# Gate weights of the first mixture: three tiles looked up first, all of them two tiles later

## The chip, the cores and the metric

The kernel runs on one core of a Trainium2 chip. The metric is the device time of one execution in microseconds; before the change it is 932.36 us, the median of 3 runs (931.68 to 932.57). TensorE (PE) multiplies matrices, VectorE (DVE), ScalarE (ACT) and GpSimd (POOL) work element by element, and SyncE (SP) issues most transfers. Each engine has a queue of its own and executes it in the order in which it is written; engines wait for each other by semaphores.

## The reference

Three layers follow each other over 2304 tokens of 512 numbers: an attention in which each row keeps only scores within tau of its maximum, and two mixtures of eight experts. Only the first mixture matters here:

```python
logits = x @ w_gate
e_idx = np.argmax(logits, axis=1)
probs = softmax(logits)                       # over the 8 experts
gate_w = probs[np.arange(N), e_idx]
eom = 1.0 / (1.0 + np.exp(-(x @ w_output_gate)))
for e in range(E):
    mask = e_idx == e
    h = np.maximum(x[mask] @ w1[e], 0.0)
    out[mask] = gate_w[mask, None] * eom[mask, e, None] * (h @ w2[e])
```

So each token goes to one expert, and its result is scaled by one number, the product of two gates.

## The kernel before

Attention fills the first third of the program. Near its end the routing of the first mixture is computed: for each token its expert and its rank among that expert's tokens, and from these its place in a list that is sorted by expert and cut into tiles of 128 places (`NT1=25` tiles at most, each of one expert). The tokens stand in 21 columns of 128 (`NC`; column 15 is empty).

Places are looked up with one-hot matrices on TensorE. For a column of tokens, `OB` says which of the 128 rows of a tile a token goes to, and `OA` which of the 25 tiles; twenty matmuls, one for each filled column, add up in PSUM to a value for every place (`onehots`, line 169). `OA` has three parts beside each other, so that three values are looked up at once (75 columns): at first the two halves of the token number and a one. So that the gathers can start early, the first three tiles are looked up from a small one-hot tile, `O3` (9 columns), before the big one (lines 151 to 154).

The first mixture (`moe1`, line 560) works tile by tile. For tile t the rows of x are gathered and transposed (`xT`), multiplied with the first weights (`mm1`, into H), passed through relu, transposed again (`hT`), multiplied with the second weights (`mm2`, into Y), scaled by the gates (`ey`, line 665, which also stores them), and transposed for the logits of the second mixture (`yT`, `logits`). Precision is kept by splitting each number into a rounded part and a rest (`xh` and `xl`, `wh` and `wl`); ScalarE rounds, VectorE (now and then POOL) subtracts, and three matmuls replace one. The tiles are interleaved: in the pass for tile t stand half of `mm1(t+1)`, `ey(t-1)`, `hT(t)`, the other half of `mm1(t+1)`, `yT(t-1)`, `xT(t+2)` and then `mm2(t)`, with the weight splits between them (lines 730 to 762). The kernel is scheduled by hand: the order in which the code runs is the order of every queue. There is one PSUM buffer for Y, so `mm2(t)` can't start until `ey(t-1)` has read it, and three for all transposes and lookups (`psT`).

The gates are computed while the first tiles run. `gates` (line 209) is a generator in three parts: exponentials and sums, right after the first tile's `mm1`; the quotient `gr`, and its split into three bf16 numbers `gb`, in the pass for tile 0; and in the pass for tile 1, ahead of `hT(1)`, the conversion of `gb` into PSUM and the three products that put the gate values into `OA` (lines 227 and 228). Later in the same pass, `gather_gates` does twenty lookups of 75 columns and adds the three parts (line 234). Then `rts.close()` gives back the routing's memory, the buffers for y are opened, and `ey(0)` scales tile 0.

Of the kernel before, what the change touches and what calls it, by code (L numbers as in the profile page):

```python
# [9 lines left out]
F32 = mybir.dt.float32  # L10
F32R = mybir.dt.float32r
BF16 = mybir.dt.bfloat16
I32 = mybir.dt.int32
AF = mybir.ActivationFunctionType
ALU = mybir.AluOpType
AX = mybir.AxisListType
ET = mybir.EngineType
P = 128
NT1 = 25
GL = 2  # L20
NC = 21
# [21 lines left out]
class Route:  # L43
# [8 lines left out]
    def T(self, nm, sh, dt=F32):  # L52
        return self.p.tile([P]+sh,dt,name=nm)
# [35 lines left out]

    def part(self, c0, c1, H=None):  # L90

# [7 lines left out]
        wt=self.wt8; vt=self.vtok[:,c]  # L99
        if H is not None:  # L100
            wt=H[:,0:8]; vt=H[:,8:8+n]; mx=H[:,32:32+n]; m2=H[:,64:64+n]
            V.tensor_copy(wt,self.wt8); V.tensor_copy(vt,self.vtok[:,c])
        def choose():
# [5 lines left out]
            V.tensor_mul(oh,t0,B8(vt))  # L109
            if H is not None: V.tensor_copy(self.mx[:,c],mx)  # L110
        def ahead(rtile):
            R[0]=rtile()[:,:8*n+8].rearrange("p (c e) -> p c e",e=8)
            for a in range(c0): nc.tensor.matmul(R[0],K['onesb'],self.oh[:,a:a+1].to_broadcast([P,n+1,8]),start=a==0,stop=False,skip_group_check=True)
# [21 lines left out]
    def tiles(self, rtile, p, mid):  # L135

        nc=self.nc; V=nc.vector; K=self.K; cst=self.cst; T=lambda nm,sh,dt=F32: p.tile([P]+sh,dt,name=nm)
        t1=T("ft1",[NC,8]); V.tensor_mul(t1,self.oh[:,:NC],self.bs.unsqueeze(1).to_broadcast([P,NC,8]))
        a=self.m2; V.tensor_reduce(a,t1,axis=AX.X,op=ALU.add)
        V.tensor_add(a,a,self.q)  # L140
        self.ix=cst.tile([P,NT1],I32,name="ix1"); self.vs=cst.tile([P,NT1],F32,name="vs1"); self.ix0=self.ri[:,:3]
        def hot(OA,n):
            B=lambda x: x.unsqueeze(2).to_broadcast([P,NC,n])
            V.tensor_tensor(OA[:,:,2],K['iota'][:,:n].unsqueeze(1).to_broadcast([P,NC,n]),B(a),op=ALU.is_equal)
            yield
            for i in range(2): V.tensor_mul(OA[:,:,i],OA[:,:,2],B(self.tok[:,i]))
            yield
        def token(ix,IX,n):
            fx=T(f"fx{n}",[n]); V.tensor_copy(fx,IX[:,1])
            V.scalar_tensor_tensor(ix,IX[:,0],16.0,fx,op0=ALU.mult,op1=ALU.add)  # L150
        O3=T("O3",[NC,3,3],BF16); h3=hot(O3,3); next(h3); next(h3)
        I3=self.onehots(rtile,O3,3)
        h=hot(self.OA,NT1); next(h)
        token(self.ix0,I3,3)

        f8=T("f8",[8]); f1=T("f1",[1]); ce=self.ce; self.tab0=self.ab[:,0,:2]
        V.tensor_scalar(f8,ce,ce[:,0:1],None,op0=ALU.is_le)
        V.tensor_scalar(self.tab0[:,1:2],ce[:,0:1],ce[:,7:8],None,op0=ALU.is_lt)
        V.tensor_reduce(f1,f8,axis=AX.X,op=ALU.add)
        V.tensor_scalar_min(self.tab0[:,0:1],f1,7.0)  # L160
        mid()
        next(h)
        IX=self.onehots(rtile,self.OA,NT1)
        tb=self.table(T); next(tb)
        token(self.ix,IX,NT1)
        V.tensor_copy(self.vs,IX[:,2])
        next(tb)
# [41 lines left out]
    def gates(self, rtile):  # L209

        nc=self.nc; V=nc.vector; T=self.T; n=NC; OA=self.OA
        dd=T("dd",[n,8]); V.tensor_sub(dd,self.LG[:,:,0:8],self.mx.unsqueeze(2).to_broadcast([P,n,8]))
        og=T("og",[n,8]); V.tensor_mul(og,self.oh[:,:n],self.LG[:,:,8:16])
        nc.scalar.activation(dd,dd,AF.Exp)
        ogs=T("ogs",[n]); V.tensor_reduce(ogs,og,axis=AX.X,op=ALU.add)
        sg=T("sg",[n]); nc.scalar.activation(sg,ogs,AF.Exp,scale=-1.0)
        yield
        se=T("se",[n]); V.tensor_reduce(se,dd,axis=AX.X,op=ALU.add)
        V.tensor_scalar_add(sg,sg,1.0)
        V.scalar_tensor_tensor(se,se,1e-9,sg,op0=ALU.add,op1=ALU.mult)  # L220
        gr=T("gr",[n]); V.reciprocal(gr,se)
        gb=T("gb",[3,n],BF16)
        for i in range(3):
            V.tensor_copy(gb[:,i],gr)
            if i<2: V.tensor_sub(gr,gr,gb[:,i])
        yield
        H=rtile()[:,:3*n].rearrange("p (i t) -> p i t",i=3); V.tensor_copy(H,gb)
        for i in range(3): V.tensor_mul(OA[:,:,i],OA[:,:,2],H[:,i].unsqueeze(2).to_broadcast([P,n,NT1]))
        yield

    def gather_gates(self, rtile):

        GX=self.onehots(rtile,self.OA,NT1); self.gs=self.cst.tile([P,NT1],F32,name="gs")
        self.nc.vector.tensor_reduce(self.gs,GX.rearrange("p i t -> p t i"),axis=AX.X,op=ALU.add)


def attention(tc, K, route, q, k, v, tau, wg, wo, xd, yz, preload):
    nc=tc.nc
    ident=K['ident']; NB=4; DIRECT=4; LG=route.LG
    with ExitStack() as ctx, ExitStack() as early:  # L240
# [293 lines left out]
        rank(); hot()  # L534
        choose,ahead,count,rank,hot=route.part(16,NC,psS.tile([P,2,512],F32,tag="S",name="H")[:,0])
        early.close()
# [23 lines left out]
def moe1(tc, K, r, rts, xd, w1, w2, wg2, ys, LG2, reach_, ahead):  # L560
# [4 lines left out]
    with ExitStack() as ctx:  # L565
# [30 lines left out]
        rtile=lambda: psT.tile([P,512],F32,tag="T",name="Tr")  # L596
# [16 lines left out]
        def gather(t):  # L613
            x=xp.tile([P,512],F32R,tag="x",name="x"); X[t]=x
            nc.gpsimd.indirect_dma_start(out=x.bitcast(F32),out_offset=None,in_=xd,in_offset=bass.IndirectOffsetOnAxis(ap=(r.ix0 if t<3 else ix)[:,t:t+1],axis=0))
# [21 lines left out]
        def relu(t):  # L637
            H=Hs.pop(t)
            h=hp.tile([P,8,P],F32,tag="h",bufs=1,name="h")
            for i in range(2): nc.scalar.activation(h[:,4*i:4*i+4],H[:,i],AF.Relu)  # L640
            Hs[t]=h
# [28 lines left out]
        def yT(t,b,i):  # L670
            y=X.pop(t)
            p=psT.tile([P,4,P],F32,tag="T",name="Ty")
            for c in range(4): nc.tensor.transpose(p[:,c],y[:,c*P:(c+1)*P],ident)
            if i==0: YT[b]=yp.tile([P,4,GL,P],F32,tag="yT",bufs=2,name="yT")
            nc.scalar.copy(YT[b][:,:,i],p)
# [35 lines left out]
        def splits(ahead):  # L711

            nonlocal pos
            while pos<min(used+ahead,ends[cur[0]]):
                t,c=order[pos]; pos+=1
                if c==0: regload(t)
                if t==0 and c<6: prefetch(t,c)
                else: split(t,c)
# [4 lines left out]
        gates=r.gates(rtile); pre=None  # L723
        splits(5); relu(0)
        next(gates)
        cnt=yp=WG=gs=None
        def run(j):
            nonlocal cnt,yp,WG,gs,pre
            t0,t1=runs[j]; lb=None; cur[0]=j; top=[]
            for t in range(t0,t1):  # L730
                i=(t-t0)%GL; b=t-i; nx=t+1<t1
                if t==t0 and j>0: splits(7); mm1(t,0,4); relu(t)
                early=t==1
                splits(5 if early else 7)
                if nx: mm1(t+1,0,2)
                if early: next(gates)
                elif t>t0: ey(t-1)
                if len(top) in (1,3): top.pop(0)()
                late=hT(t,early)
                splits(4 if early else 7)  # L740
                if t==0: next(gates)
                if nx: mm1(t+1,2,4); relu(t+1)
                if early:
                    r.gather_gates(rtile); gs=r.gs
                    rts.close()
                    yp=pool("yp",3); WG=yp.tile([P,4,32],F32,name="WG",bufs=1)
                    nc.gpsimd.memset(WG,0.0); nc.sync.dma_start(WG[:,:,:8],wg2.rearrange("(c p) e -> p c e",p=P))
                    ey(0); late(); splits(4)
                elif t>t0: yT(t-1,b if i else b-GL,(i-1)%GL)
                if t+3<N: gather(t+3)  # L750
                if t+2<N: xT(t+2)
                if lb is not None: logits2(lb,GL); lb=None
                splits(8 if nx else 7)
                end=j==0 and t==t1-1
                if end: lb=b-GL; logits(lb,GL)
                mm2(t)
                if early: yT(0,0,0)
                if t>t0 and i==0 and not end: lb=b-GL; logits(lb,GL)
                if end: pre=ahead(r.ix,r.vs,rtile)
                if j==0 and t==t1-4: top=list(reach(b-GL))  # L760
                if len(top) in (2,4,5): top.pop(0)()
                if j==0 and t==15: cnt=nc.values_load(tab[0:1,5,0:1],min_val=1,max_val=N)
            ey(t)
            if j+1<len(runs):
                with tc.If(cnt>t1,preferred_fallthrough_block=False): run(j+1)
            yT(t,b,i)
            if lb is not None: logits2(lb,GL)
            if j==0: logits1(t); next(pre)
            else: logits(b,i+1); logits2(b,i+1)
# [361 lines left out]
```

## Time and profile before

| | |
|---|---|
| median of 3 runs | 932.36 us (931.68 to 932.57) |
| profiled execution | 930.74 us, span of its instructions 928.6 us |
| mean granted TensorE clock | 0.982 of full speed |
| PE busy | 879.3 us, 95% of the span |
| DVE / ACT / POOL busy | 698.1 / 632.6 / 272.8 us |
| first mixture, from the first `mm1` | 336.1 us into the span |
| second mixture's first matmul | 692.2 us |

The profile is of one execution. Times in the rows are microseconds from the start of the span. A timeline row has start, duration, engine, line, operation, output<-inputs and the number of instructions merged into it; in square brackets how long the engine stood idle before it and what ended that. PE rows are matmuls, whose ends are modelled, so successive starts say more than durations; PEld rows are the loads of their weights.

### The profile page before, as it was taken

What the parts mean: (1) busy time and instruction counts of PE and PEld (TensorE: products, weight loads), DVE (VectorE), ACT (ScalarE), POOL (GpSimd) and SP (SyncE); (2) the same over time, 40 slices, a digit from 0 to 9 for tenths busy, and PEclk for the clock granted to TensorE, in tenths of its full rate; (3) what the DMA queues carried; (4) which work ended last, traced back from release to release, by engine and by line L of the source; (5) the groups of instructions that cost most, each with busy time, mean ns of one, the idle gap of its engine ahead of it and who ended that gap; (6) DMA issues with size and microseconds to landing.
All of it is one profiled execution on the core that took longest, in us unless ns stands there. A gap on an engine that the chain in (4) does not pass through costs nothing. (4 is left out here: it accounts for less than half of the span.)

```text
span 928.6 us, 18051 instructions
## 1 busy us (share of the span) xinstructions
PE 879.3 (95%) x5939; PEld 732.7 (79%) x5939; DVE 698.1 (75%) x1232; ACT 632.6 (68%) x1070; POOL 272.8 (29%) x350
## 2 busy tenths in 40 slices
PE   7899999999999999999999999997879999999995
PEld 6677777777777667888888888885449999999994
DVE  5998888889888789888888888887855555555540
ACT  5787878987877677888888888882324555455541
POOL 4234424432341421332233332331040222122211
PEclk9999999999999999999999999998779999999998
DMA  7534544444432572145543654112445665666400
GB/s 194 151 90 115 126 118 118 129 113 113 116 85 64 189 265 70 58 161 194 193 145 137 218 191 159 47 35 62 157 143 179 197 204 171 194 192 195 158 27 25
DMA packets 69346, 127.64 MB, mean 137 GB/s; under 512 B 14912, under 2 KB 27200, under 8 KB 69248
## 3 DMA queue, kind: packets, MB, share of 16 engines
q1 hardware_dynamic: 64016, 109.91, 38.7%
q0 software_dynamic: 5232, 16.52, 5.7%
q8 instruction: 49, 0.80, 0.4%
q14 instruction: 49, 0.40, 0.1%
HBM read 159.70 MB, written 15.99 MB: 189 GB/s over the span
## 5 line engine op out<-in xcount | busy, mean ns | idle before, releaser
L611 DVE TENSOR_TENSOR wl<-raw,wh 128x1024 fp32r<-128x1024 f32 x156 | 187.9, 1256 | 23.7 <-ACT wh L609 21.2
L609 ACT CAST wh<-raw 128x1024 fp32r x178 | 175.8, 1068 | 0.6 <-DMA raw<-in_moe_w_dram 0.4
L469 ACT ACTIVATE e<-S,nm 128x576 f32<-128x576 f32 x144 | 107.6, 748 | 55.1 <-DVE nm L464 54.7
L464 DVE TENSOR_REDUCE nm<-S 128x1 f32<-128x576 f32 x144 | 108.4, 757 | 21.9 <-PE S L388 11.2
L499 DVE SCALAR_TENSOR_TENSOR a<-S,th,e 128x576 f32<-128x576 f32 x144 | 114.4, 814 | 11.0 <-ACT e L469 4.7
L610 POOL TENSOR_TENSOR wl<-raw,wh 128x1024 fp32r<-128x1024 f32 x22 | 63.4, 2882 | 197.4 <-ACT wh L609 91.1
L966 DVE TENSOR_TENSOR wl<-raw,wh 128x1024 fp32r<-128x1024 f32 x60 | 73.4, 1225 | 36.8 <-ACT wh L966 36.8
L397 PE MATMUL T<-ident,a 128*128 128x128 f32 x576 | 86.6, 273 | 0.0
L1008 PE MATMUL H<-xh,wh 128*128 128x288 f32 x256 | 77.8, 304 | 0.1
L1020 PE MATMUL Y<-hh,wh 128*128 128x288 f32 x256 | 77.6, 303 | 0.0
L419 PE MATMUL O<-aT,v 128*64 128x288 f32 x512 | 75.8, 419 | 0.5 <-ACT xt L424 0.5
L633 PE MATMUL H<-wh,xh 128*128 128x512 f32 x184 | 75.1, 408 | 0.9 <-ACT xh L621 0.9
L1009 PE MATMUL H<-xl,wh 128*128 128x288 f32 x256 | 75.7, 296 | 0.2 <-DVE xl L1002 0.2
L1021 PE MATMUL Y<-hl,wh 128*128 128x288 f32 x256 | 75.6, 295 | 0.0
L1022 PE MATMUL Y<-hh,wl 128*128 128x288 f32 x256 | 75.5, 295 | 0.0
L1010 PE MATMUL H<-xh,wl 128*128 128x288 f32 x256 | 75.4, 294 | 0.0
L402 ACT COPY aT<-T 128x512 f32<-128x512 f32 x128 | 75.1, 587 | 0.2 <-PE T L397 0.2
L660 PE MATMUL Y<-wh,hh 128*128 128x512 f32 x184 | 73.9, 401 | 0.9 <-DVE y L667 0.9
L1037 POOL DMA_INDIRECT out_dram<-o,it x24 | 22.4, 932 | 173.1 <-ACT o L1031 154.2
L635 PE MATMUL H<-wh,xl 128*128 128x512 f32 x184 | 72.2, 392 | 0.0
L662 PE MATMUL Y<-wh,hl 128*128 128x512 f32 x184 | 71.9, 391 | 0.0
L634 PE MATMUL H<-wl,xh 128*128 128x512 f32 x184 | 71.7, 390 | 0.0
(344 smaller groups left out, 2089.4 us busy)
## 6 DMA issues: line engine op xcount, KB each, us to landing
raw<-in_moe_w_dram SPq DMA_DIRECT2D x256, 512.0 KB
ys<-y SPq DMA_DIRECT2D x23, 256.0 KB
q<-in_q_dram SPq DMA_DIRECT2D x16, 256.0 KB
k<-in_k_dram SPq DMA_DIRECT2D x16, 256.0 KB
v<-in_v_dram SPq DMA_DIRECT2D x16, 256.0 KB
QA<-QH SPq DMA_DIRECT2D x32, 128.0 KB
QB<-QH SPq DMA_DIRECT2D x32, 128.0 KB
xd<-xr SPq DMA_DIRECT2D x16, 256.0 KB
```

The costliest lines, as they stand in the source:

```text
L397: for kb in (2*part,2*part+1): nc.tensor.transpose(TT[n][:,kb,:],a[:,o+kb*P:o+(kb+1)*P],ident)
L419: nc.tensor.matmul(O[hd*64:hd*64+64,:288],L['v'][:,hd,kb,:],aT[hd][:,kb,cs],start=kb==0,stop=False,skip_group_check=True)
L464: nc.vector.tensor_reduce(nm[:,i:i+1],S[i][:,:,:288],axis=AX.XY,op=ALU.max,negate=True)
L469: nc.scalar.activation(e[i],S[i][:,:,:288],AF.Exp,bias=nm[:,i:i+1])
L499: nc.vector.scalar_tensor_tensor(a[:,hd*576:hd*576+576].rearrange("p (a b) -> p a b",a=2),S[i][:,:,:288],th[:,i:i+1],e[i],op0=ALU.is_ge,op ...
L609: nc.scalar.copy(h,rv(c,q['a']))
L611: else: nc.vector.tensor_sub(l,rv(c,q['v']),h.bitcast(F32))
L1008: nc.tensor.matmul(H[:,:288],wh[:,fs],xh[:,kc],start=kc==0,stop=False)
L1009: nc.tensor.matmul(H[:,:288],wh[:,fs],xl[:,kc],start=False,stop=False)
L1020: nc.tensor.matmul(Y[:,:288],wh[:,ds_],h,start=f==0,stop=False)
L1021: nc.tensor.matmul(Y[:,:288],wh[:,ds_],l,start=False,stop=False)
L1022: nc.tensor.matmul(Y[:,:288],wl[:,ds_],h,start=False,stop=f==7)
```

## The change

`O3` is no longer a tile of its own in memory that ends with attention, but a view of `t0`, a scratch tile of the routing that lives until `rts.close()`. The third part of `gates` becomes two: first the conversion and the three products on `O3` (3 tiles, 63 elements a row), and, when asked again, the conversion and the three products on `OA` (25 tiles, 525 elements). `gather_gates` takes the one-hot tile and its number of tiles and returns the scales. In the pass for tile 1 only those of tiles 0 to 2 are looked up (9 columns a matmul); in the pass for tile 3, behind `yT(2)`, both steps for all tiles follow each other directly, and the routing's memory is given back there.

```diff
-        O3=T("O3",[NC,3,3],BF16); h3=hot(O3,3); next(h3); next(h3)
+        O3=self.O3=self.t0.rearrange("p a b -> p (a b)").bitcast(BF16)[:,:9*NC].rearrange("p (c i t) -> p c i t",c=NC,i=3); h3=hot(O3,3); next(h3); next(h3)
...
-        H=rtile()[:,:3*n].rearrange("p (i t) -> p i t",i=3); V.tensor_copy(H,gb)
-        for i in range(3): V.tensor_mul(OA[:,:,i],OA[:,:,2],H[:,i].unsqueeze(2).to_broadcast([P,n,NT1]))
-        yield
-
-    def gather_gates(self, rtile):
-
-        GX=self.onehots(rtile,self.OA,NT1); self.gs=self.cst.tile([P,NT1],F32,name="gs")
-        self.nc.vector.tensor_reduce(self.gs,GX.rearrange("p i t -> p t i"),axis=AX.X,op=ALU.add)
+        for O,m in ((self.O3,3),(OA,NT1)):
+            H=rtile()[:,:3*n].rearrange("p (i t) -> p i t",i=3); V.tensor_copy(H,gb)
+            for i in range(3): V.tensor_mul(O[:,:,i],O[:,:,2],H[:,i].unsqueeze(2).to_broadcast([P,n,m]))
+            yield
+
+    def gather_gates(self, rtile, O, n):
+
+        GX=self.onehots(rtile,O,n); gs=(self.p if n<NT1 else self.cst).tile([P,n],F32,name=f"gs{n}")
+        self.nc.vector.tensor_reduce(gs,GX.rearrange("p i t -> p t i"),axis=AX.X,op=ALU.add)
+        return gs
...
                 if early:
-                    r.gather_gates(rtile); gs=r.gs
-                    rts.close()
+                    gs=r.gather_gates(rtile,r.O3,3)
...
                 elif t>t0: yT(t-1,b if i else b-GL,(i-1)%GL)
+                if t==3: next(gates); gs=r.gather_gates(rtile,r.OA,NT1); rts.close()
```

On VectorE in the pass for tile 1, before: the last weight subtraction, the conversion, three products on `OA`, the subtraction for the first half of h, the reduction `gs`, and the scaling of Y.

```order
L611 TENSOR_TENSOR wl<-raw_4552,wh 128x1024 [waits DMAHW5_49,Activation_49]
L227 CAST Tr<-gb 128x63 [waits DVE_49]
L228 TENSOR_TENSOR OA<-OA,Tr 128x21x25 [waits DVE_49]
L228 TENSOR_TENSOR OA<-OA,Tr 128x21x25
L228 TENSOR_TENSOR OA<-OA,Tr 128x21x25 [waits DVE_49]
L650 TENSOR_TENSOR hl<-Th,hh 128x512 [waits Activation_49]
L234 TENSOR_REDUCE gs<-Tr 128x25 [waits PE_49]
L667 TENSOR_SCALAR y<-Y,gs 128x512 [waits DVE_49]
```

The same place now; `t_930` is `t0` as the small one-hot tile.

```order
L613 TENSOR_TENSOR wl<-raw_4552,wh 128x1024 [waits DMAHW5_49,Activation_49]
L228 CAST Tr<-gb 128x63 [waits DVE_49]
L229 TENSOR_TENSOR t_930<-t_930,Tr 128x21x3 [waits DVE_49]
L229 TENSOR_TENSOR t_930<-t_930,Tr 128x21x3
L229 TENSOR_TENSOR t_930<-t_930,Tr 128x21x3 [waits DVE_49]
L652 TENSOR_TENSOR hl<-Th,hh 128x512 [waits Activation_49]
L235 TENSOR_REDUCE gs_5282<-Tr 128x3 [waits PE_49]
L669 TENSOR_SCALAR y<-Y,gs_5282 128x512 [waits DVE_49]
```

The instructions are as many and in the same order; only their shapes are smaller. In the pass for tile 3, VectorE's queue has these rows now: two weight subtractions, the conversion, the products on `OA`, the reduction, and the subtraction for x of tile 5. Before, the last of them came straight behind the second subtraction.

```order
L613 TENSOR_TENSOR wl<-raw_4555,wh 128x1024 [waits DMAHW7_49,Activation_49]
L607 TENSOR_LOAD tab
L613 TENSOR_TENSOR wl<-raw_4548,wh 128x1024 [waits DMAHW0_49,Activation_49]
L228 CAST Tr<-gb 128x63 [waits DVE_49]
L229 TENSOR_TENSOR OA<-OA,Tr 128x21x25 [waits DVE_49]
L229 TENSOR_TENSOR OA<-OA,Tr 128x21x25
L229 TENSOR_TENSOR OA<-OA,Tr 128x21x25 [waits DVE_49]
L235 TENSOR_REDUCE gs_5770<-Tr 128x25 [waits PE_49]
L623 TENSOR_TENSOR xl<-Tx,xh 128x512 [waits Activation_49]
```

Five VectorE rows are new here. On TensorE, the same pass, before: the transposes of y, those of x, those of the logits, and the first matmul of the second layer.

```order
L673 MATMUL Ty<-ident,y 128x128 [waits DVE_49,Activation_49]
L673 MATMUL Ty<-ident,y 128x128 x3
L619 MATMUL Tx<-identr,x 128x128 [waits DMASW7_49,DVE_49]
L619 MATMUL Tx<-identr,x 128x128 x3
L684 MATMUL Tl<-ident,ls 128x128 [waits DVE_49]
L684 MATMUL Tl<-ident,ls 128x128
L660 MATMUL Y<-wh,hh 128x512 [waits Activation_49]
```

And now, from the same transposes of y; eighteen more pairs of weight load and lookup stand where the rows are left out.

```order
L675 MATMUL Ty<-ident,y 128x128 [waits DVE_49,Activation_49]
L675 MATMUL Ty<-ident,y 128x128 x3
L172 LDWEIGHTS OB [waits DVE_49]
L172 MATMUL Tr<-OA,OB 128x75 [waits PE_49]
L172 LDWEIGHTS OB
L172 MATMUL Tr<-OA,OB 128x75
...
L621 MATMUL Tx<-identr,x 128x128 [waits DMASW7_49,Activation_49]
L621 MATMUL Tx<-identr,x 128x128 x3
L686 MATMUL Tl<-ident,ls 128x128 x2
L662 MATMUL Y<-wh,hh 128x512
```

Twenty lookups, the first with a wait for VectorE, now stand between the transposes of y and those of x. In tile 1 TensorE keeps its twenty lookups, with 9 columns instead of 75. The queues of ScalarE, POOL and SyncE have the same rows as before.

## Rows read from the trace of the kernel before

**Rows 1.** The page: TensorE's share, and its clock in 40 slices.

```profile
PE 879.3 (95%) x5939; PEld 732.7 (79%) x5939; DVE 698.1 (75%) x1232; ACT 632.6 (68%) x1070; POOL 272.8 (29%) x350
...
PEclk9999999999999999999999999998779999999998
```

**Rows 2.** Windows: length, then busy us (instructions) of each engine, clock, DMA.

```profile
358.00:372.00 14.00, 12.93 (x79) 10.59 (x78) 13.52 (x17) 11.63 (x16) 3.50 (x3) 1.00 0.14 40
385.00:398.00 13.00, 13.00 (x68) 10.93 (x68) 12.44 (x14) 11.70 (x16) 5.32 (x3) 1.00 0.45 152
398.00:411.00 13.00, 13.00 (x72) 10.34 (x71) 9.27 (x11) 9.85 (x14) 3.34 (x2) 1.00 0.26 92
```

**Rows 3.** Waits of TensorE's matmuls, 345 to 640 us: total, times, longest.

```profile
PE Ty L673 <- DVE A L698: 1.1, 1, 1.1
PE Y L660 <- DVE y L667: 0.9, 1, 0.9
PE Tr L172 <- DVE OA L228: 0.2, 1, 0.2
```

**Rows 4.** Timeline of the pass for tile 1, from the conversion on.

```profile
358.88 0.22 DVE L227 CAST Tr<-gb 128x63 f32<-128x63 bf16 x1
359.13 2.05 DVE L228 TENSOR_TENSOR OA<-OA,Tr 128x525 bf16<-128x525 bf16 x3
...
361.23 0.89 PE L172 MATMUL Tr<-OA,OB 128*128 128x75 bf16 x20 [0.20 <-DVE OA L228]
...
361.95 0.51 PE L619 MATMUL Tx<-identr,x 128*128 128x128 f32 x4
...
362.16 0.24 DVE L234 TENSOR_REDUCE gs<-Tr 128x25 f32<-128x75 f32 x1 [0.38 <-PE Tr L172]
...
362.43 0.75 DVE L667 TENSOR_SCALAR y<-Y,gs 128x512 f32<-128x512 f32 x1
...
363.33 0.47 PE L660 MATMUL Y<-wh,hh 128*128 128x512 f32 x1 [0.87 <-DVE y L667]
```

**Rows 5.** Timeline around the routing's lookups from the small tile.

```profile
328.03 0.39 DVE L146 TENSOR_TENSOR O<-O,tok 128x63 bf16<-128x63 bf16 x2
...
328.96 0.66 PE L172 MATMUL R<-O,OB 128*128 128x9 bf16 x20
...
329.65 0.16 DVE L149 COPY fx<-R 128x3 f32<-128x3 f32 x1 [0.65 <-PE R L172]
```

**Rows 6.** Timeline of the pass for tile 3.

```profile
384.13 2.36 DVE L611 TENSOR_TENSOR wl<-raw,wh 128x1024 fp32r<-128x1024 f32 x2 [1.72 <-ACT wh L609]
...
388.26 2.72 DVE L611 TENSOR_TENSOR wl<-raw,wh 128x1024 fp32r<-128x1024 f32 x2
...
389.13 0.60 PE L673 MATMUL Ty<-ident,y 128*128 128x128 f32 x4
...
389.49 0.54 PE L619 MATMUL Tx<-identr,x 128*128 128x128 f32 x4
...
391.42 0.69 DVE L621 TENSOR_TENSOR xl<-Tx,xh 128x512 fp32r<-128x512 f32 x1 [0.43 <-ACT xh L621]
```

**Rows 7.** Timeline at two waits of TensorE.

```profile
24.61 0.50 PE L387 MATMUL S<-XA,QA 128*128 128x288 f32 x2 [1.61 <-DVE a L499]
...
681.23 2.43 PE L900 MATMUL IX<-OT,OR 128*96 128x48 bf16 x25 [3.61 <-POOL OT L896]
```

**Rows 8.** Windows in the second routing, columns as in rows 2.

```profile
665.50:668.50 3.00, 2.19 (x28) 1.16 (x27) 2.60 (x10) 2.05 (x3) 0.00 (x0) 1.00 0.00 0
669.00:672.00 3.00, 3.00 (x6) 1.36 (x6) 2.90 (x12) 0.58 (x1) 0.00 (x0) 0.51 0.00 0
672.50:675.00 2.50, 2.25 (x33) 1.19 (x31) 1.54 (x9) 0.58 (x1) 0.00 (x0) 1.00 0.01 3
676.00:679.00 3.00, 1.46 (x26) 1.37 (x26) 2.41 (x14) 0.00 (x0) 0.00 (x0) 1.00 0.00 0
679.50:689.00 9.50, 6.88 (x35) 3.63 (x35) 3.86 (x9) 0.79 (x1) 4.59 (x5) 0.50 0.75 266
```

## The prediction

> **What bounds the kernel now.** I read the page's busy shares first: TensorE is busy for 95% of the span, and the slices show its clock at 9 tenths or more nearly throughout [rows 1]. Then I cut the first mixture into its tiles: from 385 to 411 us TensorE is busy for 13.00 of every 13.00 us at full clock, VectorE for 12.44 and 9.27 [rows 2]. In the 295 us from 345 to 640 the waits that TensorE's matmuls show are a handful: 1.1, 0.9 and 0.2 us are the longest [rows 3]. So in this stretch TensorE sets the end, work that hides under it is worth nothing, and each microsecond in which its queue stands is lost for good: the engines execute their queues in the written order, and what comes later (second routing, second mixture) starts from its results.
>
> **The change part by part.** Two places on two engines change, tile 1 and tile 3.
>
> *Tile 1, less work.* Before, VectorE converts the split weights in 0.22 us and runs three products on the 525-element one-hot tile, 2.05 us together, TensorE's twenty lookups of 75 columns start at 361.23 after waiting 0.20 us for the last product, the reduction starts at 362.16, the scaling of tile 0's output at 362.43, and the first matmul of the second layer, which needs the accumulator freed, at 363.33 after a wait of 0.87 us [rows 4]. Now the products run on the 63-element tile. Two products of that shape took 0.39 us [rows 5], so three take some 0.6 us instead of 2.05, and the 0.20 us wait goes: lookups at 361.03. For twenty lookups of 9 columns the trace has the first routing: they start at 328.96, and the VectorE step that waits for them starts at 329.65, 0.69 us later [rows 5]. That puts the reduction at 361.72, the scaling 0.27 us behind it at 361.99, and the matmul 0.90 us behind that at 362.89: 0.44 us earlier than 363.33. The bounds: 0.20 us if only the product wait goes, and 1.3 us if all of TensorE's idle time from 358 to 372 us (14.00 less 12.93, so 1.07) went and 0.2 us of lookup time with it (0.89 against 0.66 us for the twenty [rows 4, 5]). I take 0.45, near the row-by-row chain. The 1.4 us that VectorE gains there is not counted: behind it VectorE runs ahead of a TensorE that doesn't wait for it.
>
> *Tile 3, the moved work.* The conversion, three full products, twenty lookups of 75 columns and the reduction now stand here, with nothing between the products and the lookups. On VectorE they come behind the two weight subtractions that start at 388.26 and take 2.72 us, so until 390.98 [rows 6]. From the start of the conversion to the first lookup it was 361.23 less 358.88, 2.35 us [rows 4]: first lookup at 393.33. TensorE reaches that place after the four transposes of y, which start at 389.13; the transposes of x, the next work on its queue, started at 389.49 [rows 6]. Twenty lookups hold the queue for 0.72 us (361.23 to 361.95 [rows 4]), so the transposes of x start at 394.05: 4.56 us late, 3.6 of it standing still. Queued behind the waiting weight load on TensorE are those transposes, the transposes of the logits and all of the second layer of tile 3; ScalarE's rounding of x and VectorE's subtraction, which started at 391.42 [rows 6], wait for the first of them, and every later weight split waits behind these in the two engines' queues. All three engines are late by about the same, so nothing catches up: VectorE and ScalarE have slack against TensorE, but TensorE has none against itself. Bounds of this term: if POOL's traffic no longer stretches the two subtractions (2.72 against 2.36 us for the pair that starts at 384.13) it is 4.2; with one more subtraction's worth of delay on VectorE (half of that pair, 1.2 us) it is 5.8.
>
> *The rest.* Keeping the small tile in other memory costs VectorE nothing: same instructions, same order. The output buffers opened before the routing memory is released add no wait on any queue, and no DMA moves.
>
> The sum at full clock is 4.56 less 0.45: 4.1 us late.
>
> *The clock.* A standstill of 3.6 us has one counterpart in this trace: the lookups of the second routing waited 3.61 us, until 681.23 [rows 7]. The clock was 1.00 from 676 to 679, and 0.50 (1.2 instead of 2.4 GHz) from 679.5 on, so it fell inside the wait, and it stayed at 0.50 until 689 [rows 8]. Before that wait TensorE had been thinly used (1.46 of 3.00 us), which here it has not; but the length is the same, and the fall came with the wait half over. I hold a fall for likelier than not. What it costs can be read where the clock fell ahead of dense work: it was 1.00 until 668.5, 0.51 from 669 to 672 with TensorE busy for all of the 3.00 us, and 1.00 again from 672.5 [rows 8]. So 3.0 to 4.0 us were worked at half rate, and 1.5 to 2.0 us lost. Bounds: nothing, if the clock holds; 3.9 us, if it stays low for the 7.8 us from 681.23 to 689 with TensorE saturated. I take 1.8, the row with dense work.
>
> Sum: 4.1 and 1.8, 5.9 us. The profiled execution took 930.74 us, 2.1 around its span of 928.6; it would take 936.6. The median of the three timed runs is 1.6 us above it, 932.36, and so the forecast for the median is 938.3 us.
>
> **The rivals.**
>
> *The clock holds.* Then it is 4.1 us alone: 936.5 us. For it: TensorE is saturated on both sides of the gap, and at the start of attention a wait of 1.61 us up to 24.61 [rows 7] left that slice's clock at 9 tenths or more [rows 1]. Against it: that wait was less than half as long, and the one of this length saw a fall. The Trainium skill, in "TensorE: Matmul & The Clock Gate", section "Loop structure matters more than you think", counts a VectorE step between two tiles' matmuls as harmless to the clock, and a long wait as what makes them cold. By its first half this rival would come true; but in its good loop the matmuls don't wait for that step, and the fall within the 3.61 us wait, which was one for POOL, speaks for the second half.
>
> *The clock stays low for long.* As after 681.23: 4.1 and 3.9, 940.4 us. Against it: TensorE had little to do behind that wait at first, while behind this gap the work is dense, as from 669 on, where the clock was back within 4 us.
>
> *VectorE is through in time* (the other side). If VectorE had finished the products when TensorE has done the transposes of y, only the 0.72 us of lookups would be added, less 0.45 to 1.3 at tile 1: between 931.8 and 932.6 us, no slower than before. The point from which it decides: the products would have to end by 389.49, so the two subtractions by 387.1 instead of 390.98, 3.9 us earlier. For it: VectorE loses 1.4 us of work in tile 1. Against it: it doesn't keep them. Before the pair at 384.13 it stands 1.72 us for ScalarE's rounded weights [rows 6], which follow TensorE; what VectorE gains in tile 1 becomes a longer wait there.
>
> **How the numbers follow.** The forecast, gap with a fall of the clock, has 0.60; the clock that holds 0.25; the clock that stays low 0.06; VectorE in time 0.09, of which a little would be measurably faster. A difference of 0.2%, 1.9 us, is about what a measurement of this kernel can tell from no change. The three slow cases lie 4 us and more above, so slower has 0.90, same 0.07, faster 0.03. The range reaches from the holding clock with the smallest gap term and the larger gain (4.2 less 1.3, so 2.9 us late: 935.2) to the long low clock (940.4).
>
> **What would show it.** In the profile after, TensorE's first lookup of tile 3 shows a wait of some 3.6 us put down to the third product, and the transposes of x start some 4.1 us later against the transposes of h of tile 1 than before. The first second-layer matmul of tile 1 waits some 0.4 instead of 0.87 us. The granted clock is 0.50 for some microseconds around the gap, or it is not: that tells the forecast from its nearest rival. If TensorE shows no wait above 1 us at tile 3, the forecast is wrong at its largest term; if it shows it and the time is within 2 us of before, something later absorbed it, against rows 3.

## The result, and the profile after

The changed kernel takes 941.38 us (median of 4 runs, 940.86 to 942.13) against 932.02 us before (4 runs, 931.30 to 932.57): ratio 1.0100, 95% interval 1.0085 to 1.0115. It is slower, as forecast, but by 9.4 us where 5.9 were forecast, and the time lies above the range. The profiled execution took 942.13 us, the longest of the four; its span is 940.0 us and its mean granted clock 0.975.

Tile 1 first, the timeline of the kernel after (columns as in [rows 4], to which it answers; its lines have numbers two higher).

```profile
359.49 0.67 DVE L229 TENSOR_TENSOR t<-t,Tr 128x63 bf16<-128x63 bf16 x3
...
361.29 0.66 PE L172 MATMUL Tr<-t,OB 128*128 128x9 bf16 x20
...
361.78 0.40 PEld L621 LDWEIGHTS Tx<-identr,x 128*128 128x128 f32 x4
361.80 0.51 PE L621 MATMUL Tx<-identr,x 128*128 128x128 f32 x4
361.98 0.17 DVE L235 TENSOR_REDUCE gs<-Tr 128x3 f32<-128x9 f32 x1 [1.25 <-PE Tr L172]
362.18 0.75 DVE L669 TENSOR_SCALAR y<-Y,gs 128x512 f32<-128x512 f32 x1
...
363.08 0.47 PE L662 MATMUL Y<-wh,hh 128*128 128x512 f32 x1 [0.76 <-DVE y L669]
```

The three products take 0.67 us instead of 2.05. From the start of the first `mm1` (336.50 here, 336.14 before) to the last row it is 0.61 us less than before; 0.45 was forecast. The wait in the last row is 0.76 us where some 0.4 were forecast: TensorE's transposes of x, the work ahead of it, come 0.51 us sooner after the first `mm1` than before, and so TensorE reaches the wait sooner too.

Tile 3, which answers to [rows 6].

```profile
388.04 2.72 DVE L613 TENSOR_TENSOR wl<-raw,wh 128x1024 fp32r<-128x1024 f32 x2
...
388.91 0.60 PE L675 MATMUL Ty<-ident,y 128*128 128x128 f32 x4
...
390.69 0.21 DVE L228 CAST Tr<-gb 128x63 f32<-128x63 bf16 x1
390.94 2.05 DVE L229 TENSOR_TENSOR OA<-OA,Tr 128x525 bf16<-128x525 bf16 x3
...
393.04 1.45 PE L172 MATMUL Tr<-OA,OB 128*128 128x75 bf16 x20 [3.54 <-DVE OA L229]
...
394.29 0.73 PE L621 MATMUL Tx<-identr,x 128*128 128x128 f32 x4
...
395.67 0.69 DVE L623 TENSOR_TENSOR xl<-Tx,xh 128x512 fp32r<-128x512 f32 x1 [0.91 <-ACT xh L623]
```

TensorE is done with the transposes of y and stands 3.54 us for the third product; 3.6 was forecast. The windows of the same stretch (columns as in [rows 2]) show what the clock did.

```profile
391.00:392.00 1.00, 0.00 (x0) 0.00 (x0) 1.00 (x2) 0.00 (x0) 0.00 (x0) 0.73 0.71 213
391.40:398.20 6.80, 5.16 (x33) 4.54 (x34) 4.19 (x8) 2.61 (x4) 0.00 (x0) 0.51 0.33 108
398.30:401.00 2.70, 2.70 (x13) 2.23 (x12) 2.19 (x3) 1.86 (x2) 0.00 (x0) 1.00 0.66 211
```

It fell inside the wait, to 1.2 GHz, and came back 5.2 us after the first lookup had started. Up to the last matmul of the first mixture's last tile the kernel is now 6.3 us late, counted from the first `mm1`. So far that is the forecast.

The rest of the loss is at a place that the forecast does not name: the end of the first mixture. There the program asks whether there are more tiles than the usual 23 (the `If` on `cnt`, after the loop), and each engine's sequencer executes a conditional branch. The branch's two instructions on TensorE, before (L765) and after (L767); the columns are min, median and max in ns, then the first and the last start.

```profile
L765 PEldq COMPARE_BRANCH  x2: 98/208/319, 637.7 to 642.1; - x2
```

```profile
L767 PEldq COMPARE_BRANCH  x2: 98/1926/3753, 644.3 to 648.8; - x2
```

The one that ends last takes 3753 instead of 319 ns. TensorE's waits from the branch on, before and then after, put the same time at the first matmul behind it ("issue": no releaser that the profile shows).

```profile
PE cn L836 <- DVE G L832: 6.0, 4, 3.2
PE IX L900 <- POOL OT L896: 3.6, 1, 3.6
PE sp L858 <- DVE gp L857: 1.2, 5, 0.2
PE Ty L673 <- DVEq L765: 1.0, 1, 1.0
...
PE L L689 <- issue: 0.5, 1, 0.5
```

```profile
PE cn L838 <- DVE G L834: 6.0, 4, 3.2
PE Ty L675 <- issue: 4.1, 1, 4.1
PE IX L902 <- POOL OT L898: 3.6, 1, 3.6
```

In the stretch of the branch, 648.6 to 652.7 us, the DMA view of the kernel after has a packet of q8, one of two queues that the page calls "instruction". On the page of the whole execution this queue has 49 packets in 0.80 MB, 16 KB each; in the trace of before TensorE starts some 245 instructions on average from one of them to the next.

```profile
DMA packets 146, 0.29 MB, mean 70 GB/s; under 512 B 16, under 2 KB 16, under 8 KB 144
...
q8 instruction: 1, 0.02, 1.4%
```

Before has such a packet too, so the packet alone is not the loss: it starts 1.07 us behind the start of the branch's second instruction there (643.16) and 1.34 us behind it in the kernel after (650.09). What differs is TensorE meanwhile. Before, it goes on, and only the last of the eight matmuls of line 689 waits, the 0.5 us for "issue" above. After, the branch itself ends at 652.50, 1.49 us behind the end of the packet (651.01).

The table gives, for each kernel run here, how late its profile is against that of before, in us, at the first `mm1`, at the first second-layer matmul of tiles 2 and 4 (between them lies all of the moved work), at the last one of all, at the transposes of the last y behind the branch (`Ty`), at the lookups of the second routing (`IX`) and at the second mixture's first matmul. Up to the first `mm1` e1, e7 and e8 run the code of before, and yet lie 0.08 to 1.66 us behind it, so the steps between columns say more than the last column.

| kernel | `mm1` | tile 2 | tile 4 | last | `Ty` | `IX` | 2nd mixture |
|---|---|---|---|---|---|---|---|
| after | 0.35 | -0.22 | 6.62 | 6.66 | 9.78 | 11.15 | 11.35 |
| e1_pad40 | 0.08 | 0.06 | 0.61 | 0.62 | 3.36 | 4.78 | 4.69 |
| e2_late | 1.00 | 0.37 | 2.32 | 2.37 | 5.31 | 6.31 | 6.21 |
| e3_fill | 1.25 | 1.16 | 5.69 | 5.68 | 5.69 | 6.42 | 8.97 |
| e4_short | 0.92 | 0.40 | 6.50 | 6.53 | 6.53 | 7.58 | 7.51 |
| e5_late_short | 0.99 | 2.10 | 4.08 | 4.08 | 4.08 | 4.13 | 3.92 |
| e6_fill_short | 0.20 | 0.39 | 4.86 | 4.93 | 4.93 | 6.08 | 6.11 |
| e7_pad68 | 1.23 | 1.16 | 2.18 | 2.20 | 2.20 | 2.08 | 5.36 |
| e8_pad20 | 1.66 | 1.56 | 1.85 | 1.93 | 1.93 | 4.89 | 6.63 |
| e9_rotate | 0.86 | 1.98 | 3.34 | 3.40 | 3.41 | 3.88 | 3.80 |

### The profile page after: what moved, and what is told of

Read it like the earlier page. It is cut to its first block, busy times and chain, and to the rows that moved or that the text cites. A ratio compares the mean times of both kernels' runs of the same rounds, so it can differ in the third digit from the quotient of the medians.

```text
span 940.0 us, 18096 instructions
## 1 busy us (share of the span) xinstructions
PE 884.0 (94%) x5959; PEld 736.3 (78%) x5959; DVE 699.3 (74%) x1237; ACT 633.6 (67%) x1070; POOL 272.3 (29%) x350
## 5 line engine op out<-in xcount | busy, mean ns | idle before, releaser
L663 PE MATMUL Y<-wl,hh 128*128 128x512 f32 x184 | 72.2, 392 | 0.0
```

## The experiments

The theory for the second loss: the change adds 20 lookups, each a weight load and a matmul, so 40 instructions, to TensorE's code ahead of the branch. All later code moves by so much, and the branch meets a load of code that came a little later before. Its rival: the branch is late because something that it waits for is late, as a consequence of the standstill and the clock at tile 3.

**e1_pad40: the shift alone.** The kernel before, with twenty tiny matmuls in the pass for tile 3 and nothing else.

```diff
+        def tiny(n):
+            w=psT.tile([P,512],F32,tag="T",name="tiny")
+            for _ in range(n): nc.tensor.matmul(w[:,:9],K['onesb'],K['onesb'][:,:9],start=True,stop=True)
...
+                if t==3: tiny(20)
```

> The kernel before, with twenty tiny matmuls (9 columns, result unused) behind yT(2) in the pass for tile 3: as many TensorE instructions more as the change adds (20 weight loads, 20 matmuls), but no wait for VectorE and no products moved. Theory 'code place': the conditional branch behind the last tile takes 3.75 instead of 0.32 us because the code it jumps to has moved by 40 TensorE instructions; the branch takes 3 to 4 us here too, and the time is 932.0 + 0.5 for the matmuls + 3.4 to 4.1 = 936 to 936.7 us. Rival 'lateness' (the branch is slow because the engines arrive late or the routing's memory is given back late): the branch takes 0.3 us and the time is 932.5.

Measured: 936.31 us (10 runs) against 931.71, ratio 1.0033 (1.0015 to 1.0052). Its branch and the wait behind it:

```profile
L769 PEldq COMPARE_BRANCH  x2: 98/1736/3373, 638.3 to 642.7; - x2
```

```profile
PE Ty L673 <- issue: 3.7, 1, 3.7
```

Without any moved work, and 0.62 us late when it reaches the end of the mixture, the kernel spends 3.4 us in the branch and is 3.36 us late behind it. The shift of the code is enough for it. Three of the ten executions took 930.6, 931.0 and 933.0 us, so they seem not to pay; the profiled one does, and why the others don't is open.

**e2_late: no standstill.** The kernel after, with the lookups of all tiles behind the second layer of tile 3, so that TensorE has work while VectorE makes the products.

```diff
-                if t==3: next(gates); gs=r.gather_gates(rtile,r.OA,NT1); rts.close()
+                if t==3: next(gates)
...
                 mm2(t)
+                if t==3: gs=r.gather_gates(rtile,r.OA,NT1); rts.close()
```

> The changed kernel, with the twenty full lookups and their reduction behind mm2(3) instead of directly behind the products; as many TensorE instructions. Theory: TensorE no longer stands 3.5 us for the products and its clock doesn't fall there (6.8 us at half rate, so 3.4 us lost, go too): 941.4 less 6.9 = 934.5 us, with the slow branch (3.75 us) kept, since the code has not moved. Rival 'the clock fall costs little by itself': 941.4 less 3.5 to 5.3 = 936 to 938. Rival 'lateness': the branch is fast again, 931 us.

Measured: 936.21 us (10 runs), ratio 1.0038 (1.0023 to 1.0053), above the 934.5 expected. The standstill is gone, and tile 2 to tile 4 cost 1.95 us instead of 6.84; the branch is as slow as in the kernel after, 3573 ns. So the branch does not hang on the standstill: the rival falls. The 1.95 us are some 0.8 of lookups and a new wait:

```profile
391.31 0.44 PE L686 MATMUL Tl<-ident,ls 128*128 128x128 f32 x2 [0.93 <-ACT yT L677]
```

The converted gates (`gb`) take one of the three PSUM buffers of `psT` now, ahead of the transposes of x and of the logits. The reading, which e9 puts to the test: the logits' transposes get the buffer from which ScalarE is still copying y.

**e3_fill: the clock held.** The kernel after, with 14 matmuls of 512 columns in the gap, between products and lookups.

```diff
+            for _ in range(n): nc.tensor.matmul(w,K['onesb'],K['onesb'].unsqueeze(1).to_broadcast([P,4,P]),start=True,stop=True)
...
-                if t==3: next(gates); gs=r.gather_gates(rtile,r.OA,NT1); rts.close()
+                if t==3: next(gates); fill(14); gs=r.gather_gates(rtile,r.OA,NT1); rts.close()
```

> The changed kernel, with 14 matmuls of 512 columns (3.0 us, result unused) put on TensorE's queue between yT(2) and the lookups, where it stands 3.5 us. The lookups still start when the products are done. Theory: the clock holds at 1.00 around tile 3, and the loss by half rate goes: 941.4 less 3.4 = 938.0 us (less 1.8, 939.6, if the fall costs what the prediction took for it). Rival 'the clock is a bystander': 941.4. The 28 instructions more move the code again; the branch's own duration tells what that does.

Measured: 939.17 us (4 runs), ratio 1.0070 (1.0051 to 1.0088). The windows at tile 3 and the largest "issue" wait of TensorE:

```profile
391.00:395.00 4.00, 3.50 (x30) 1.71 (x29) 3.29 (x5) 1.05 (x3) 0.84 (x1) 1.00 0.45 145
395.00:402.00 7.00, 7.00 (x43) 5.91 (x40) 5.79 (x8) 6.01 (x7) 0.00 (x0) 1.00 0.49 164
```

```profile
PE w L1048 <- issue: 4.2, 1, 4.2
```

The clock stays at 2.4 GHz, and tile 2 to tile 4 cost 4.53 us: the standstill and the lookups alone. The first branch is not slow here. Instead TensorE stands 4.2 us behind the second routing's branch, ahead of the second mixture. Its code is 68 instructions longer than before, not 40.

**e4_short: the shift undone.** The kernel after, with 40 TensorE instructions fewer at its start: in the warm-up matmuls, twenty pairs of 256 columns become single ones of 512.

```diff
-            for _ in range(n): nc.tensor.matmul(w[:,:256],BDL[1][:,0],BDH[1].rearrange("p a b -> p (a b)"),start=True,stop=True)
+            B=BDH[1].rearrange("p a b -> p (a b)"); wide={18:8,20:10,10:2}.get(n,0)
+            for _ in range(wide): nc.tensor.matmul(w,BDL[1][:,0],B.unsqueeze(1).to_broadcast([P,2,256]),start=True,stop=True)
+            for _ in range(n-2*wide): nc.tensor.matmul(w[:,:256],BDL[1][:,0],B,start=True,stop=True)
```

> The changed kernel, with 20 fewer matmuls (40 TensorE instructions) in the warm-ups at the start, where pairs of 256 columns are replaced by single ones of 512: the code behind stands where it stood before the change, tile 3 is untouched. Theory 'code place': the branch takes 0.3 us and the time is 941.4 less 3.4 to 4.1 = 937.3 to 938.0 us. Rival 'lateness': the branch still takes 3.75 us, 941.4.

Measured: 938.67 us (4 runs), ratio 1.0069 (1.0048 to 1.0090). Its branch, and its waits from 345 to 660 us:

```profile
L769 PEldq COMPARE_BRANCH  x2: 98/208/319, 644.2 to 648.6; - x2
```

```profile
PE Tr L172 <- DVE OA L229: 3.5, 1, 3.5
...
PE Ty L677 <- DVEq L769: 1.0, 1, 1.0
```

The standstill stays, the branch is back at 319 ns, and the wait behind it is the 1.0 us of before. With e1 this settles the second loss from both sides: the shift alone costs 0.33%, the change without the shift 0.69%; together 1.02%, and 1.00% was measured. (The tiny matmuls of e1 cost 0.55 us in tiles 2 to 4 by themselves, some 0.06%.)

**e5_late_short: both mends.** e2's and e4's edits together.

> The changed kernel with both mends: lookups of tile 3 behind mm2(3), and 40 TensorE instructions fewer in the warm-ups. Theory (standstill, clock fall and code place are the whole loss): no wait over 0.3 us at tile 3, clock 1.00 there, branch 0.3 us; against before 0.61 us gained at tile 1 and 0.72 us lost on the lookups: 931.7 + 0.1 = 931.8 us, ratio 0.999 to 1.001. Rival 'something else is late too': 934 us or more.

Measured: 934.12 us (9 runs) against 931.89, ratio 1.0024 (1.0014 to 1.0034); 931.8 was expected. Standstill and slow branch are both gone. What is left at tiles 2 to 4, 1.98 us, is the 0.9 us wait for the buffer, which 931.8 does not contain, and the lookups. Another 1.11 us are lost from the first `mm1` to tile 2, where the kernel after gains 0.57. In the first tile TensorE stands 0.8 us for a weight split of VectorE (`wl`), VectorE waits for ScalarE's rounding, and ScalarE for a transfer of the weights: 2.0 us in two waits from 337 to 352 us, 0.4 before. Up to there the program is that of e4, which shows no such wait and gains 0.52 us; what makes the transfer land later was not tried.

**e6_fill_short: the standstill by itself.** e4's mend, with 48 instructions fewer, and four full-precision matmuls of 512 columns in the gap, written as in e3 (`ident` for `onesb`). In the trace the four are eight matmuls and eight weight loads, 3.60 us together. So they fill the gap, not half of it as planned, and the code behind stands 8 instructions later than before, not in its place.

> The changed kernel, lookups in their place, with 4 matmuls of 512 columns in full float32 (some 0.5 us each, 1.8 to 2.0 us, result unused) on TensorE's queue inside the standstill, and 48 TensorE instructions fewer in the warm-ups (so the code behind stands where it stood before the change, and the 8 more of the filling are made up for). It shows the price of the standstill alone. Theory: clock 1.00 around tile 3, branch 0.3 us, 931.7 + 4.5 - 0.6 = 935.6 us. If half-filling doesn't hold the clock, 937.3 to 939.

Measured: 937.47 us (4 runs), ratio 1.0064 (1.0049 to 1.0080); 935.6 was expected. The windows at tile 3:

```profile
391.00:395.00 4.00, 3.91 (x33) 2.12 (x33) 2.76 (x6) 0.35 (x2) 0.08 (x1) 1.00 0.47 134
395.00:402.00 7.00, 7.00 (x33) 5.80 (x32) 6.33 (x7) 6.42 (x7) 0.24 (x1) 1.00 0.51 177
```

The clock holds, the branch takes 319 ns, and tile 2 to tile 4 cost 4.47 us: that is the term of 4.56 by itself, for the lookups still start when the last product has ended (at 393.6 us), and not later for the filling. Against it the clock's share is 2.4 us in the kernel after (6.84) and 1.6 in e4 (6.10). By the times it is less certain: e4 and e6 are 0.69% and 0.64% above before, and their intervals overlap. Of the 1.9 us above the expectation 1.15 arise between `Ty` and `IX`, where one more wait of 1.1 us for "issue" stands; 0.5 us of it are there before as well (the same matmuls, L689), and 0.8 in e4.

```profile
PE L L693 <- issue: 1.1, 1, 1.1
```

**e7_pad68 and e8_pad20: other shifts.** e1 with 34 and with 10 tiny matmuls, so 68 and 20 instructions (`tiny(34)`, `tiny(10)`).

> The kernel before with 34 tiny matmuls at tile 3 (68 TensorE instructions more, the shift that the filled kernel had). Theory 'code place': the branch behind the last tile is fast (0.3 to 0.4 us), and TensorE stands some 4 us without a releaser at the end of the second routing instead, in front of the matmuls that keep it busy: 931.7 + 0.9 + 3.5 = 936.1 us. Rival 'the filled kernel's second standstill came from something else': 932.6 us.

> The kernel before with 10 tiny matmuls at tile 3 (20 TensorE instructions more). Theory 'code place': the price is a step, not a slope: the branch takes either 0.3 us (932.0 us) or some 3.4 (935.5), not half of it. A slope would be 1.7 us more, 933.7.

Measured: e7 935.66 us (5 runs), ratio 1.0036 (1.0021 to 1.0050); e8 934.83 us (5 runs), ratio 1.0029 (1.0016 to 1.0043). The first and the second branch of e7, and the wait behind the second:

```profile
L769 PEldq COMPARE_BRANCH  x2: 98/252/406, 639.9 to 644.3; - x2
...
L941 PEldq COMPARE_BRANCH  x2: 64/2013/3962, 685.6 to 686.1; - x2
```

```profile
PE w L1047 <- issue: 4.4, 1, 4.4
```

This is e3's picture without e3's work: at 68 instructions the second branch pays. In e8 the first branch takes 319 ns, and the wait stands one row of the program further, behind the transposes of y (timeline of e8):

```profile
644.82 0.63 PE L673 MATMUL Ty<-ident,y 128*128 128x128 f32 x4 [0.99 <-DVEq L769]
...
648.14 0.66 PE L684 MATMUL Tl<-ident,ls 128*128 128x128 f32 x2 [2.70 <-issue]
```

For e8 neither of the expected cases came: the branch is fast and the time is lost all the same. All three shifts tried with a pad cost 0.3% to 0.4%, while before pays 0.5 us behind the branch.

The kernels together show where TensorE is stopped. In each of them a packet of q8 starts 1.0 to 1.3 us behind the start of the branch at the first mixture's end, and wherever TensorE waits for "issue" at this place, the wait ends 1.4 to 1.5 us behind the end of that packet. With the code in the place of before (before, e4, e5, e9) it is the 27th or 28th TensorE instruction behind the branch, loads and matmuls counted, that waits; with 8 more ahead (e6) it is the 21st, with 20 more (e8) the 9th, and with 40 more (after, e1, e2) the branch itself. So the place moves ahead by as many instructions as were added, give or take two, and the sooner TensorE comes to it, the longer it stands. That the packet brings the code from this place on is read from these times; no run shows it apart.

**e9_rotate: the mended change.** e5, with the conversion and the products behind the logits of the pass for tile 3, so that the logits' transposes keep the buffer that they had before.

```diff
-                if t==3: next(gates)
                 if t+3<N: gather(t+3)
                 if t+2<N: xT(t+2)
                 if lb is not None: logits2(lb,GL); lb=None
+                if t==3: next(gates)
```

> The changed kernel with both earlier mends (lookups of all tiles behind the second layer of tile 3, forty TensorE instructions fewer in the warm-up at the start), and the conversion and the three products on VectorE behind the logits of that pass instead of ahead of the transposes of x, so that the logits' transposes no longer get the PSUM buffer that ScalarE is still reading for y. Theory (the wait of 0.93 us there comes from the order in which the three PSUM buffers are handed out): that wait goes, the kernel with both mends is 0.9 us faster, 933.2 us, and level with the kernel before within 0.2%: what is left is the second set of lookups, some 0.8 us, against 0.6 us won at tile 1. Rival (that wait covers another, for VectorE or ScalarE, which then appears in its place): no gain, 934.1 us or more. That it beats the kernel before is expected by neither.

Measured: 933.77 us (11 runs) against 932.32 (15 runs), ratio 1.0009 (1.0000 to 1.0019). In its timeline the logits' transposes follow those of x without a wait:

```profile
391.46 0.54 PE L623 MATMUL Tx<-identr,x 128*128 128x128 f32 x4
...
391.83 0.41 PE L688 MATMUL Tl<-ident,ls 128*128 128x128 f32 x2
...
392.00 0.48 PE L664 MATMUL Y<-wh,hh 128*128 128x512 f32 x1
```

So the buffer's rotation was the wait, as the theory had it. The ratio fell by 0.15% against e5, of which the wait explains 0.1%; the two intervals meet. With all three causes mended the change is level with the kernel before, and not clearly faster or slower. Its profile loses 1.11 us up to tile 2 as e5's does, by the same wait:

```profile
PE H L638 <- DVE wl L615: 0.8, 1, 0.8
```

Another 1.36 us go between tiles 2 and 4, some 0.8 of them in the second set of lookups, which is more than the 0.6 gained in tile 1. Five of the eleven executions took 931.8 to 932.6 us and six 933.8 to 934.7; the profiled one (934.42) is of the six. Whether the five lack the wait in the first tile is not shown.

## Why the prediction was wrong, step by step

- **The bound.** TensorE sets the end of this stretch; right. What it stands at tile 3 is still missing 240 us later: from tile 4 to the last tile the lateness moves from 6.62 to 6.66 us.
- **Tile 1, 0.45 us gained.** Right: 0.61. The sign named for it, a wait of some 0.4 us ahead of the second layer, did not come (0.76).
- **Tile 3, 4.56 us.** Right in mechanism and size: a standstill of 3.54 (3.6 forecast) and, with the clock held, 4.47 and 4.53 us in e6 and e3. The rival in which VectorE is through in time fell: its pair of subtractions started at 388.04 (388.26 before), so of the 1.4 us gained in tile 1 little was left by then.
- **The clock, 1.8 us.** Right in kind: it fell inside the wait, and 2.4 us were lost in the profiled execution (1.6 in e4). The rival in which it holds became true only with the gap filled. The Trainium skill, in "TensorE: Matmul & The Clock Gate", section "Loop structure matters more than you think", counts a VectorE step between tiles as harmless and a long wait for DMA between the matmuls as what makes them cold; the 0.51 from 391.4 to 398.2 agrees with the second half, but here the wait was one for VectorE.
- **The rest, nothing: this step failed.** The prediction costed the edits by what TensorE, VectorE and the queues execute, and nothing for the place of the code behind them. In its paragraph on tile 3 the twenty added lookups are counted, as 0.72 us of work; that they are also 40 instructions, and that a branch 260 us later answers to their number, was not considered. It costs 3.1 us in the profile after (from the last second-layer matmul to `Ty`), and 0.33% alone (e1). The median is 3.1 us above the forecast too, but that the two are equal is chance: profile against profile the kernel is 11.4 us late (928.6 to 940.0) where 5.9 were forecast, and the 5.5 us between are 3.1 at the branch, 1.6 behind it, 0.4 ahead of the first mixture and 0.4 in it.
- **Behind it.** From `Ty` to the second mixture another 1.6 us went in the profile after, which the sum did not have either: 1.3 in e1, which has the slow branch alone, 1.0 and 1.2 in e4 and e6 with a fast one. In the kernel after the clock is at half speed for longer there; a window of before, and one of after:

```profile
646.00:658.00 12.00, 7.03 (x59) 3.93 (x57) 9.76 (x42) 2.00 (x4) 0.00 (x0) 0.50 0.83 293
```

```profile
651.00:667.00 16.00, 9.06 (x70) 6.67 (x71) 9.04 (x40) 2.45 (x5) 0.00 (x0) 0.50 0.75 263
```

  It is 0.50 for 12 us before and for 16 us after. That is not all of it: e4 is at half speed for some 10 us there (0.62 from 654 to 655, 0.50 to 664, 0.76 to 665) and loses 1.0 us all the same. What sets this length in the thinly used stretch was not tried apart.

What stays open: why some executions of e1 and e2 seem not to pay at the branch; which count of instructions would be free, since only +20, +40 and +68 were tried (and +8 in e6, with the moved work); where the last 1.6 us come from; and why the first tile of e5 and e9 waits for its weights.

## What to carry to other kernels

When an edit adds or removes instructions on an engine whose queue is full, count them and look at the later branches of that engine: compare the branch's duration, and the "issue" waits behind it, before and after. A small pad without any work tells such a loss from a loss in the moved work. And where a step is moved, give the engine that waits for it something else first (here the second layer ahead of the lookups), and look whether its scratch buffer takes the turn of another one.

## What was not expected of the hardware

- A conditional branch on TensorE took 319 ns or 3.4 to 4.0 us (3373, 3573, 3753 and 3962 ns) in otherwise equal code, by the number of instructions ahead of it: 0, 8 and 20 more gave 319 ns at the first branch, 40 more 3373 to 3753 ns, 68 more 406 ns and then 3962 ns at the second. With 0, 8 and 20 more TensorE waited some instructions behind the branch instead, for 0.5 to 0.8, 1.1 and 2.7 us.
- A wait of 3.5 us for VectorE between dense matmuls brought the clock from 1.00 to 0.51; matmuls without use in that gap (14 in e3; 4 in e6, which the trace shows as 8) kept it at 1.00, and left the time of the stretch at the wait itself.
